# Seven products for the last pair of batches, and the layers of the pair before it moved behind attention

## The chip, the cores and the metric

The kernel runs on one core of a Trainium2 chip. Its engines work side by side, each through its own queue in order: TensorE (PE in the profile, with its weight loads as PEld), VectorE (DVE), ScalarE (ACT), GpSimd (POOL) and SyncE (SP), which only issues transfers. GpSimd issues the indirect transfers (gathers and scatters by a list of row numbers). Engines wait for each other by semaphores. The metric is the device time of one execution in microseconds; the kernel before takes 687.97 us (median of 3 runs, 686.82 to 688.27).

## The reference, cut to what matters

Attention comes first, with the queries averaged in pairs, for 8 batches of 8 heads, 1152 keys, and heads of 64:

```
q_pool = q.reshape(B, H, S // 2, 2, D).mean(axis=3)          # 576 queries
attn   = softmax(q_pool @ k^T / sqrt(D))                     # 576 x 1152
x      = (attn @ v), heads side by side                      # (8, 576, 512)
```

Then each batch sends its 128 best rows through two layers, and the other rows are passed on as they are:

```
scores = einsum('bsd,d->bs', x, w_gate)
for b in range(B):
    top_idx = argpartition(-scores[b], 128)[:128]
    h  = maximum(x[b, top_idx] @ w1, 0)                      # 128 x 1024
    ye = h @ w2                                              # 128 x 512
    out[b, top_idx] += sigmoid(scores[b, top_idx])[:, None] * ye
```

So a batch's layers need its chosen rows, the choice needs the scores of all its 576 rows, and the scores need all of its attention. All arithmetic is in float32; the profile shows each float32 matmul as two instructions.

## The kernel before, in words

**Attention.** The work goes through 32 pairs of heads (`pairs`, batch by batch, four pairs each), each in two halves of 288 queries. The loop in `run` counts 64 halves with `h`. For a half, TensorE does 72 matmuls for the scores (line L869), from which ScalarE makes exponentials into a tile `p` (L876), and one half later 72 matmuls of exponentials by values (`weighted`, L887). GpSimd adds the exponentials of two thirds of the keys (L908), VectorE folds both parts to sums (`folded`, L913, twice a half, and L923), and transposes the drained result (`drained`, L966). VectorE also transposes keys and queries of the pair after the next (`prepare_pair`, L770 and L774). `p` has two buffers.

**Routing.** When a batch's last pair has been scored (`scored`), a generator `routed` is put on the list `routing`. Each `yield` ends a piece of it. `units` runs a piece at one of three places in a half ("mid", "sums", "end"), the place being given by the value that the piece before yielded. The pieces in order: the line of scores (L1068), its spreading to all partitions and to columns, comparisons of each row's score with all others (L1152, L1161, L1171 on VectorE, by tile of 128 rows) which give ranks, a transfer of the ranks to memory and back to every partition (`row_rank`, `lines`, L1201 and L1205, 640 KB), the search for the row of each rank (L1236), the gather of the chosen rows from the output (L1263), their transposition (`xeT`), and the layers.

For batches 0 to 6 the line of scores goes by way of memory (`row`, L1094, read back by L1097 to L1099). For batch 6 it is first merged over the partitions by a matmul (L1083). For batch 7 nothing of this goes by memory: VectorE spreads the line over a diagonal (L1113), two matmuls give it to all partitions (L1124, copied by L1133), five small transposes give its columns (`columns`, L679), and after the ranks a product with matmuls (L1213, L1222) gives the row numbers directly. Batch 7's rows are transposed by TensorE (L1308), the other batches' by a transfer to memory and back (`copy`, L1276 and L1292) and VectorE.

**Layers.** Batches 0 and 1, 2 and 3, 4 and 5 go through the layers as pairs (`layers_of_two`). The rows of a pair, and a weight matrix, are each cut into a two by two block of quarters, and `seven_products` makes the product of both from seven products of quarters instead of eight (L1452). For this there are sums of quarters: of the weights (`tw`, made once and kept in memory, with room in the chip for one layer's at a time, `load_sums`, L730) and of the rows (`input_sums` on GpSimd, L1418). ScalarE copies the products out of PSUM (L1460) and VectorE adds them (seven additions, L1465). Batches 6 and 7 (`b >= self.paired`) each go through `layers`: for layer 1, 32 products of 128 by 128 by 128 (L1327, with ReLU L1335), for layer 2, 8 products with 512 columns (L1347), for batch 7 in two parts of 256 columns.

**Output.** Attention's rows are stored by SP (`stored`, L1024, four transfers a pair). The changed rows are scattered over them by GpSimd (`written`, L1394), one scatter a batch, for batch 7 one for each part of 256 columns. All of them write one tensor of the output, of which `written` names the rows from the first to the end of its batch.

**The end, before.** The first layer of batches 4 and 5 is run within attention (at half `h` = 60). Behind attention the order is written out by hand at the end of `run`: `old` is the rest of batch 6's routing and layers, `older` the second layer of batches 4 and 5, and `new` batch 7's routing and layers; `pieces(unit, n)` runs n pieces. `normalized` merges the last pair's sum by a matmul (L989), and `counted` and `outside` count the softmax sums that are out of bounds, on which a branch to another version of the kernel depends (not taken here).

```
        pieces(new, 1)
        pieces(old, 1)
        for half in (halves[-3], halves[-1]):
            self.divided(half["pair"])
            self.stored(half["pair"])
        pieces(older, 2)
        pieces(new, 1)
```

In this way TensorE has the second layer of 4 and 5, then the layers of 6, to do while batch 7 is routed by the other engines.

Of the kernel before, what the change touches and what calls it, by code (L numbers as in the profile page):

```python
# [13 lines left out]
G = 3  # L14
# [520 lines left out]
class _Plain:  # L535
# [10 lines left out]
    def __init__(self, ctx, tc, q, k, v, moe_w_gate, moe_w1, moe_w2, capacity, out):  # L546
# [48 lines left out]
        self.paired = self.B - 2 - self.B % 2  # L595
        self.tw = self.const.tile([P, 4, self.ND // 2 * self.F // 2], F32, name="tw")
        self.tw_kept = {}
# [70 lines left out]
    def line_of_scores(self):  # L668

        line = self.ffn.tile([P, self.NT * P], F32, name="sc_row", bufs=1)  # L670
        self.nc.gpsimd.memset(line[0:1, self.Sp :], 0.0)
        return line

    def columns(self, to, line):

        nc = self.nc
        ps = self.banks()[:, 0, 0 : self.NT]
        for t in range(self.NT):
            nc.tensor.transpose(  # L679
                ps[:, t : t + 1], line[0:1, t * P : (t + 1) * P], self.ident[0:1, 0:1]  # L680
            )
        nc.scalar.copy(to[:, :], ps)

# [50 lines left out]

    def load_pair(self, b, hp):

        nc = self.nc
        kb = self.load.tile([P, self.KB, BLK], F32, name="kb")
        qb = self.load.tile([P, self.QB, 2, BLK], F32, name="qb", bufs=1)
# [318 lines left out]
    def routed(self, b, part):  # L1058
# [13 lines left out]
        if b < self.B - 1:  # L1072

            yield mid
            if b < self.B - 2:
                groups = self.side_by_side(line)
                yield True
                total = self.added(groups)
            else:
                yield True  # L1080
                total = self.small.tile([BLK, self.QB], F32, name="total", bufs=3)
                ps = self.banks()[:, 0, 0 : self.QB]
                nc.tensor.matmul(  # L1083
                    ps,
                    lhsT=self.merge.rearrange("p g j -> p (g j)"),
                    rhs=line[:, :],
                    start=True,
                    stop=True,
                )
                nc.scalar.copy(total[:, :], ps[0:BLK, :])  # L1090
            sc_row = ffn.tile([P, NT * P], F32, name="sc_row", bufs=1)
            row = self.dram.tile([Sp], F32, name="row")
            nc.gpsimd.memset(sc[:, NF:], 0.0)
            nc.sync.dma_start(row.rearrange("(i n) -> i n", i=BLK), total[:, :])  # L1094

            def reads():
                nc.sync.dma_start(sc_row[:, 0:Sp], _rows_of(row[:], P))  # L1097
                nc.sync.dma_start(sc[:, 0:NF], row[0 : NF * P].rearrange("(t p) -> p t", p=P))
                nc.sync.dma_start(  # L1099
                    sc[0 : self.TAIL, NF:], row[NF * P :].rearrange("(t p) -> p t", p=self.TAIL)  # L1100
                )

            if b < self.B - 2:
                self.behind_keys.append(reads)
            else:
                reads()
            yield True
            if b < self.B - 2:
                yield True
        else:  # L1110

            diag = ffn.tile([P, self.QB, BLK], F32, name="lines", bufs=1)
            nc.vector.tensor_tensor(  # L1113
                out=diag[:, :, :],
                in0=line[:, :].unsqueeze(2).broadcast_to([P, self.QB, BLK]),
                in1=self.same[:, :].unsqueeze(1).broadcast_to([P, self.QB, BLK]),
                op=ALU.mult,
            )
            yield True
            sc_row = self.line_of_scores()  # L1120

            halves = [self.banks()[:, 0, 0 : self.HALF] for _ in range(2)]
            for s, ps in enumerate(halves):
# [343 lines left out]
    def layers_of_two(self, tokens):  # L1467
# [12 lines left out]
        for _ in self.input_sums(a, s):  # L1480
            pass
# [279 lines left out]
```

## Time and profile before

| what | value |
|---|---|
| median of 3 runs | 687.97 us (686.82 to 688.27) |
| profiled execution, its own time | 687.04 us |
| its span | 685.3 us |
| TensorE busy | 676.5 us (99%) |
| VectorE busy | 564.9 us (82%) |
| GpSimd busy | 516.9 us (75%) |
| ScalarE busy | 458.5 us (67%) |
| transfers | 101.21 MB, mean 148 GB/s |
| share of the chain that ended last: TensorE | 90% |
| granted TensorE clock | 0.997 |

Busy shares are averages over the span. The chain of work that ended last is followed back from the last instruction, at each step to what released it or to the instruction before it on its engine. In the timeline a row gives start, duration, engine, line, operation, what it writes and reads, its shape, how many instructions are merged in it, and in square brackets how long the engine stood idle before it and what released it. TensorE's rows are pipelined and their ends are modelled. Times are in microseconds from the start of the span.

### The profile page before, as it was taken

The numbers are of one execution on the slowest core, as the hardware profiler recorded it, in microseconds if no ns is written. First come the engines' busy times: TensorE is split into PE (matmuls) and PEld (weight loads), VectorE is DVE, ScalarE is ACT, GpSimd is POOL, SyncE is SP. The second block draws the span as 40 slices with busy tenths as digits, with TensorE's granted clock in tenths as the row PEclk, the third lists the DMA queues.
The fourth block names the chain that finished last, engine by engine and source line by source line (L and its number), as shares of the span: only waits on it lengthen the run. The fifth ranks groups of instructions, "written<-read, shape, count | busy, mean of one in ns | idle before, by whom it ended". The sixth has DMA issues, their size and how long they took to land.

```text
span 685.3 us, 23541 instructions
## 1 busy us (share of the span) xinstructions
PE 676.5 (99%) x9972; PEld 450.9 (66%) x9972; DVE 564.9 (82%) x842; ACT 458.5 (67%) x998; POOL 516.9 (75%) x503
## 2 busy tenths in 40 slices
PE   8999999999999999999999999999999999999996
PEld 6666666666666568676666657767657665866875
DVE  3878998999999986787699996696879999688830
ACT  5677777777877783848787776583877777576220
POOL 4788888879887883857998788393999889559241
PEclk9999999999999999999999999999999999999998
DMA  8889889849986886744989687572788959344311
GB/s 157 163 179 195 217 185 195 161 91 192 206 179 108 174 156 105 193 88 85 226 192 160 139 165 158 114 175 51 166 197 185 162 123 194 71 116 119 81 47 36
DMA packets 395570, 101.21 MB, mean 148 GB/s; under 512 B 375744, under 2 KB 379712, under 8 KB 394176
## 3 DMA queue, kind: packets, MB, share of 16 engines
q1 hardware_dynamic: 393920, 95.13, 67.0%
q0 software_dynamic: 1296, 4.20, 1.9%
q8 instruction: 80, 1.31, 0.8%
q10 hardware_dynamic: 240, 0.30, 0.2%
q14 instruction: 34, 0.28, 0.1%
HBM read 81.97 MB, written 17.62 MB: 145 GB/s over the span
## 4 chain that ended last, share of the span: by engine, by line
PE 90%; POOL 4%; issue 2%; DMA 2%; DVE 1%; ACT 1%; ACTq 0%; POOLq 0%; DVEq 0%
PE ps L869 39%; PE ps L887 38%; PE ps L1452 11%; POOL acc L908 2%; PE ps L1327 1%; DMA out_dram<-xe,index 1%; POOL xe L1512 1%; DMA p<-in_q_dram 1%; POOL out_dram L1394 1%; POOL qp L767 0%; DMA out_dram<-lines,index_part 0%; POOL prod L976 0%; ACT p L876 0%; DVE kT L770 0%; POOL x L1013 0%
## 5 line engine op out<-in xcount | busy, mean ns | idle before, releaser
L876 ACT ACTIVATE p<-ps 128x576 f32<-128x576 f32 x576 | 321.0, 696 | 4.3 <-PE ps L869 4.0
L908 POOL TENSOR_TENSOR acc<-p 128x576 f32<-128x576 f32 x192 | 275.9, 1464 | 27.9 <-ACT p L876 27.6
L869 PE MATMUL ps<-qT,kT 64*64 64x288 f32 x4608 | 292.9, 403 | 1.6 <-DVE qT L774 0.9
L887 PE MATMUL ps<-p,v_sb 64*64 64x288 f32 x4608 | 291.4, 403 | 0.0
L869 PEld LDWEIGHTS ps<-qT,kT 64*64 64x64 f32 x4608 | 174.6, 133 | 107.4 <-ACT p L876 17.6
L887 PEld LDWEIGHTS ps<-p,v_sb 64*64 64x64 f32 x4608 | 174.1, 133 | 105.4 <-ACT p L876 14.0
L913 DVE TRANSPOSE_TENSOR_REDUCE fold<-p 128x54 f32<-128x1728 f32 x64 | 126.0, 1969 | 27.4 <-ACT p L876 26.8
L913 DVE TRANSPOSE_TENSOR_REDUCE fold<-acc 128x54 f32<-128x1728 f32 x64 | 124.5, 1946 | 21.1 <-POOL acc L908 20.8
L895 ACT COPY two<-ps 128x576 f32<-128x576 f32 x64 | 40.8, 637 | 135.1 <-PE ps L887 118.9
L897 POOL TENSOR_TENSOR av<-two 128x288 f32<-128x288 f32 x64 | 51.2, 800 | 81.4 <-ACT two L895 79.9
L770 DVE STREAM_TRANSPOSE kT<-kb 128x1152 f32<-128x1152 f32 x31 | 73.3, 2364 | 0.0
L976 POOL TENSOR_TENSOR prod<-avb,w_gate 128x288 f32<-128x288 f32 x64 | 51.2, 800 | 0.2
L767 POOL TENSOR_TENSOR qp<-qb 128x576 f32<-128x576 f32 x31 | 43.7, 1409 | 4.7 <-DMA qb<-in_q_dram 4.7
L966 DVE STREAM_TRANSPOSE avb<-av 128x288 f32<-128x288 f32 x64 | 28.6, 447 | 20.0 <-POOL av L897 20.0
L953 ACT ACTIVATE sums<-total,tiny 32x18 f32<-32x18 f32 x124 | 38.2, 308 | 3.0 <-DVE total L944 1.1
L1013 POOL TENSOR_TENSOR x<-avb,rec 128x576 f32<-128x576 f32 x30 | 34.7, 1157 | 0.0
L1171 DVE SCALAR_TENSOR_TENSOR pick<-sc_row,gate_sc,before 128x128 f32<-128x128 f32 (+1 forms) x40 | 32.8, 821 | 1.4
L938 ACT COPY groups<-sum 32x36 f32<-32x36 f32 x124 | 27.2, 219 | 1.5
L1035 DVE TENSOR_REDUCE red<-prod 128x9 f32<-128x288 f32 x64 | 27.7, 434 | 0.1
L1460 ACT COPY s<-ps 128x256 f32<-128x256 f32 (+1 forms) x27 | 11.4, 446 | 20.9 <-PE ps L1452 20.9
L923 DVE TENSOR_REDUCE sum<-fold 128x18 f32<-128x108 f32 x64 | 21.9, 342 | 2.2
L1460 ACT COPY hT<-ps 128x512 f32<-128x512 f32 (+1 forms) x15 | 7.9, 544 | 23.2 <-PE ps L1452 21.3
(136 smaller groups left out, 496.0 us busy)
## 6 DMA issues: line engine op xcount, KB each, us to landing
kb<-in_k_dram SPq DMA_DIRECT2D x124, 144.0 KB
qb<-in_q_dram SPq DMA_DIRECT2D x124, 144.0 KB
v_sb<-in_v_dram SPq DMA_DIRECT2D x31, 576.0 KB
tw<-tw SPq DMA_DIRECT2D x10, 1024.0 KB
out_dram<-x SPq DMA_DIRECT2D x128, 72.0 KB
lines<-row_rank SPq DMA_DIRECT2D x7, 640.0 KB
w<-in_moe_w_dram SPq DMA_DIRECT2D x8, 512.0 KB
tw<-tw SPq DMA_DIRECT2D x8, 512.0 KB
```

Source lines behind the costliest of these rows:

```text
L767: nc.gpsimd.tensor_tensor(out=qp[:, :, :], in0=pair["q"][:, :, 0, :], in1=pair["q"][:, :, 1, :], op=ALU.add)
L770: nc.vector.transpose(kT.rearrange("p (c i g) -> p c g i", c=self.NC, i=BLK), pair["k"].rearrange("p (g c) d -> p c g d", c=self.NC),)
L869: nc.tensor.matmul(sc[keys, j, 0:n], lhsT=pair["kT"][rows, c * P + keys.start : c * P + keys.stop], rhs=pair["qT"][rows, qs], start=True, ...
L876: nc.scalar.activation(p[:, c // G, c % G, :, :], sc[:, :, 0:n], AF.Exp, scale=self.scale)
L887: nc.tensor.matmul(av[j * self.D : (j + 1) * self.D, e, 0:n], lhsT=half["pair"]["v"][keys, j, c, :], rhs=half["p"][keys, c // G, c % G, j, :],
L895: nc.scalar.copy(two[:, :, :], av[:, :, 0:n])
L897: nc.gpsimd.tensor_tensor(out=half["av"][:, :], in0=two[:, 0, :], in1=two[:, 1, :], op=ALU.add)
L908: nc.gpsimd.tensor_tensor(out=acc[:, u, :], in0=units[:, 0, u, :], in1=units[:, 1, u, :], op=ALU.add)
L913: nc.vector.tensor_reduce(fold[:, a, :], of.rearrange("p u (m d) -> p (u m) d", d=BLK), AX.X, ALU.add, apply_transpose=True,)
L953: self.nc.scalar.activation(tot[rows, :], pair["total"][:, j * self.QB : (j + 1) * self.QB], AF.Identity, bias=self.tiny[0:BLK, 0:1],)
L976: self.nc.gpsimd.tensor_tensor(out=pair["prod"][:, ns, :], in0=pair["avb"][:, ns, :], in1=self.w_gate[:, hp : hp + 1, :].broadcast_to([P, ...
L1452: nc.tensor.matmul(args[0], lhsT=args[1], rhs=args[2], start=k == 0, stop=k == n - 1)
```

## The change

Four parts, all around the end of attention:

- `layers_of_two` stops for batches 4 and 5 after the sums of the input (`self.left`); both their layers are run behind attention. The marks "hidden", `waiting` and `place` that had put layer 1 inside and layer 2 outside are gone.
- Batches 6 and 7 no longer go through `layers` but, as a pair, through `first_layer` and `second_layer`, in seven products each. Here the order of the seven is another than in `seven_products`: those that need no sums first, and VectorE adds products straight from PSUM. For layer 2, `load_last_sums` loads the kept sums of the weights in four transfers of 512 KB into tiles of keys and queries during the last two pairs, so that the sums of layer 1 can stay in `tw` for both pairs.
- Batch 7's line of scores is spread by four ScalarE copies and one reduction and goes by way of `row` in memory, as the earlier batches' does; the diagonal and `columns` are gone. Batch 6's line is made by the same copies instead of the matmul. Batch 7's two small gate operations go from GpSimd to VectorE.
- The end is a function of its own, `ending`, with a new order: attention's last half, layer 1 of 4 and 5 between the pieces of batch 7's routing, the four sums of its layer 2 on GpSimd, layer 2 with the rest of the routing, then layer 1 and layer 2 of 6 and 7 with their sums on VectorE. The scatters come in the order 4, 5, first half of 6's columns, all of 7, second half of 6's columns.

The diff, cut to its core:

```diff
-            if b < self.B - 2:
-                groups = self.side_by_side(line)
-                yield True
-                total = self.added(groups)
-            else:
-                yield True
...
+        groups = self.side_by_side(line)
+        if b < self.B - 1:
             yield True
+        total = self.added(groups)
+        sc_row = ffn.tile([P, NT * P], F32, name="sc_row", bufs=1)
+        row = self.dram.tile([Sp], F32, name="row")
+        nc.gpsimd.memset(sc[:, NF:], 0.0)
+        nc.sync.dma_start(row.rearrange("(i n) -> i n", i=BLK), total[:, :])
...
-            self.columns(sc, sc_row)
...
+        small = nc.vector if b == self.B - 1 else nc.gpsimd
...
             if b >= self.paired:
-                yield mid
-                yield from self.layers(token)
+                self.last_tokens.append(token)
...
+        if tokens[1]["b"] + 1 == self.paired:
+            self.left = tokens, a, s
+            return
         yield "mid"
...
+    def load_last_sums(self):
...
+        for room in rooms:
+            to = (self.row(room) if len(room.shape) > 2 else room)[:, 0:n]
+            self.nc.sync.dma_start(to, self.tw_kept[2][:, len(self.last_sums), :])
...
+    def first_layer(self, a, s, c, m):
...
+        copy(u, product(a11, b11))
+        hidden(c11, u, product(a12, b21))
+        copy(w, product(s1, t1))
+        self.add(u, u, product(s2, t2))
+        self.add(w, w, u)
+        ps = product(s3, t3)
+        hidden(c22, w, ps)
+        self.add(u, u, ps)
+        hidden(c12, w, product(s4, b22))
+        hidden(c21, u, product(a22, t4))
...
+    def second_layer(self, a, s):
...
+        for of, by in ((a11, b11), (a12, b21), (a22, t4), (s1, t1), (s2, t2), (s3, t3), (s4, b22)):
+            yield self.product(2, of, by, self.banks()[:, 0, :])
...
+    def ending(self, halves, old):
...
+        self.gated(halves[-3])
+        pieces(old, 1)
+        self.weighted(halves[-1])
+        self.drained(halves[-1])
+        self.multiplied(halves[-2])
+        self.multiplied(halves[-1])
+        self.scored(halves[-3])
+        self.gated(halves[-2])
+        pieces(layer, 1)
+        self.normalized(last)
+        self.gated(halves[-1])
+        self.scored(halves[-1])
+        _, new, _ = self.routing.pop()
+        pieces(old, 1)
+        pieces(new, 1)
+        pieces(layer, 2)
+        for of in (halves[-3]["pair"], last):
+            self.divided(of)
+            self.stored(of)
+        pieces(layer, 3)
+        pieces(new, 1)
+        pieces(layer)
+        room = self.ffn.tile([P, 4, 512], F32, name="s", bufs=1).rearrange("p a n -> p (a n)")
+        s = self.four_sums(nc.gpsimd, c, room)
...
+        layer = self.second_layer(c, s)
+        for to in at[0:2]:
+            copy(to, next(layer))
+        pieces(new, 2)
+        for to in at[2:5]:
+            copy(to, next(layer))
+        pieces(new, 1)
+        pieces(old)
+        for to in at[5:7]:
+            copy(to, next(layer))
+        low = self.counted()
...
+        pieces(layer, 1)
+        pieces(new)
+        self.four_sums(nc.vector, a, room)
...
+        ps = next(layer)
+        add(v, v, ps)
+        add(u, u, ps)
+        scaled(to[3], v, seven, to[3])
+        add(y, y, u)
+        scaled(to[2], y, seven, to[2])
+        self.written(seven, seven["index"])
+        scaled(to[1], next(layer), six, z)
+        self.written(six, index[1], 1, 2)
```

## The prediction

> **What bounds the kernel now.** I read the page's busy shares first (busy us, share of the span, instructions), then the chain of work that ended last (start, us, what), then the timelines around the places that the diff touches.
>
> ```profile
> PE 676.5 (99%) x9972; PEld 450.9 (66%) x9972; DVE 564.9 (82%) x842; ACT 458.5 (67%) x998; POOL 516.9 (75%) x503
> ```
>
> The chain where the diff takes work out:
>
> ```profile
> 582.44 0.33 PE ps L1083 x2
> 582.77 4.53 PE ps L869 x72
> 587.29 12.70 PE ps L1452 x112
> ...
> 626.52 8.73 PE ps L887 x144
> 635.25 1.93 PE ps L1452 x8
> ```
>
> TensorE has work all the time, and the chain follows it almost to the end. 12.70 us of the first layer of batches 4 and 5 (L1452, 112 matmuls, seven products of 1.81) stand inside attention; the last weighted sum ends at 635.25. From there TensorE runs without a gap to 679.58. The granted clock is 1.00 up to 665, so matmul rows can be carried over.
>
> The edges of the last stage, and the queue that ends the kernel, from the timeline:
>
> ```profile
> 635.52 0.34 DVE L923 TENSOR_REDUCE sum<-fold 128x18 f32<-128x108 f32 x1
> 637.01 0.31 PE L989 MATMUL ps<-sum,merge 128*128 128x36 f32 x2
> ...
> 660.68 1.03 POOL L1394 DMA_INDIRECT out_dram<-xe,index  x1 [0.28 <-POOL xe L1512]
> 664.27 1.00 POOL L1394 DMA_INDIRECT out_dram<-xe,index  x1 [1.12 <-DMA out_dram<-xe,index]
> 676.99 0.98 POOL L1394 DMA_INDIRECT out_dram<-lines,index_part  x1 [8.07 <-DVE index_part L1381]
> 680.38 0.97 POOL L1394 DMA_INDIRECT out_dram<-lines,index_part  x1 [2.42 <-DVE lines L1356]
> ```
>
> Two things to see. VectorE finishes the sum of the last half only 0.6 us after attention ends on TensorE. And a scatter to the output is not started before the one ahead of it has landed: the second line of L1394 waits for a DMA, and the chain shows the landing 2.79 us after the first one's start and 0.80 more until the next starts.
>
> The last row that carries a step is a comparison (L1171) on VectorE, beside POOL's sums and without them:
>
> ```profile
> 607.71 1.43 DVE L1171 SCALAR_TENSOR_TENSOR pick<-sc_row,gate_sc,before 128x128 f32<-128x128 f32 x1
> 610.17 0.39 DVE L1171 SCALAR_TENSOR_TENSOR pick<-sc_row,gate_sc,before 128x128 f32<-128x128 f32 x1
> 617.84 1.51 DVE L1171 SCALAR_TENSOR_TENSOR pick<-sc_row,gate_sc,before 128x128 f32<-128x128 f32 x1
> ```
>
> **1. TensorE's own work.** Before, the moved and removed parts take 12.70 (layer 1 of 4 and 5) + 0.33 (merge of batch 6's line, L1083) + 44.33 (635.25 to 679.58) = 57.36 us. After: two pairs, each with 12.70 for layer 1 and 12.57 for layer 2 (the chain's four L1452 pieces after 635.25: 1.93 + 3.53 + 1.73 + 5.38), 50.54; merge 0.14 (L989), choice of rows 1.15 (L1222), transposes 0.63 (L1308), count 0.19 (L1541): 52.65. Gone are the plain layers (7.3 and 7.1 per batch by L1327 and L1347) and batch 7's line on TensorE (L1124 1.03, L679 0.40). TensorE gains 4.7 us. Attention then ends at 635.25 - 13.03 = 622.2, and without any wait TensorE would end at 674.9.
>
> **2. The cover that goes.** Those 12.70 us were time in which VectorE caught up: idle 3.07 and 1.39 us before its two folds at 588.59 and 591.96, 1.48 at 595.78, 1.67 at 606.20. Its queue from the first fold's partner (ends 593.94, bound by POOL as before) to the sum of the last half, in start-to-start times of the trace, without the seven additions L1465 (0.69 each): sum, totals, two transposes, the drained half 3.9, ranks of batch 6 5.3: 603.2. Next half 8.9, of which 1.16 was one comparison beside POOL, which now is done by then: 611.0. Next half's folds and drain 5.2: 616.2. Then it needs the 640 KB of batch 6's ranks: the write went out at 620.94 and the search that needs them began at 627.96, 7.0 later; so 618.0. Two searches: 3.3 as seen, 1.85 by their shortest rows; 2.6 taken, 620.6. Last half 4.55: 625.2. TensorE has its merge (L989) in line behind one product, at 622.2 + 1.8 = 624.1. Everything behind the merge waits with it: **1.2 us**. Ends: 623.3 (shortest searches and a transfer sooner by 1.2), no wait; 627 (another tie comparison beside POOL), 3.
>
> **3. Batch 7's line by way of memory.** I count from the sum of the last half, S. Drain, gate reductions and part take 3.6 (635.86 to 639.74 now); four ScalarE copies 0.92 and one reduction: S+4.9. The row's write to its first read: 1.42 by the row at 620.94 and its follower at 622.36, quiet queues; 3.97 (585.31 to 589.28) under full DMA load. The load is light by then, so 1.42. Three reads are issued over 0.9, and the last lands 3.0 after its issue (one such read held POOL's gate once, 362.12 to 365.4): S+10.3. Ahead of them on SP are batch 6's copy and its reading (637.83 and 640.14 now), done some 3 us before. Behind them are eight stores, 6.1 us of issue, landed by S+17, and the gather that needs them comes at S+23: free. The four loads of layer 2's sums (2 MB, as before) go out during the last two pairs and are not needed for 20 us; if late, the first product with a sum is S+16.5.
> VectorE's own queue fills the same time: two divisions 1.42, six additions of 0.69 up to the sixth product, S+10.4. So the detour costs nothing here; without that cover it would cost the difference to the matmul way (639.74 to 644.36, 4.6): about 2. PSUM as an addition's source I bound by 0.69 and 0.8 (L1356, 0.48 for 256).
>
> **4. Choice of rows of batch 7.** Ranks of tiles 0 and 1 take 2.65 and the gate 0.25: S+13.3; one addition 0.69; tiles 2 to 4, rank and choice 5.6 (647.03 to 652.56 now): S+19.7 alone. But POOL does the four sums of layer 2 (1.28 each) from S+14.9 to S+20, beside three comparisons and the choice. One or two of three are stretched by about 1.1 in the trace: 0 to 3.4, taken 1.6, so S+21.3 and 0.15 to TensorE. TensorE arrives at S + 0.3 + 6 x 1.81 + 5 x 1.80 = S+20.2. Wait: **1.25 us** (0 to 3). The sums themselves are ready 0.3 ahead of their products.
> The Trainium skill, SBUF — State Buffer, section "SBUF: two separate sides", says that a VectorE operation with two SBUF inputs and a GpSimd operation lock each other out for a whole instruction; L1171 at 607.71 agrees (1.43) and at 610.17 doesn't (0.39, with POOL busy). By the rule each of the four operations would wait half of a POOL sum, 4 x 0.64 = 2.6 instead of 1.6, and the result would be 1 us later.
> The gather then has 3.6 + 1.8 of products to land in; 654.11 to about 658.1 now, 4.0. Free; a landing of 5.5 instead of 3.5 would cost 0.6.
>
> **5. The pair 6 and 7.** Layer 1 takes additions of 0.69 on VectorE, about 9 us in 11 us of products; layer 2 starts with three products that need no sum, 5.4 us, and the first sum is ready 2.1 us after layer 1. No wait. Edits at nothing: batch 6's line by four ScalarE copies of 0.22 instead of a matmul, ScalarE being 67% busy and the line not needed for 12 us; the gate's two small operations on VectorE (0.1 each, in step 4); the count of odd sums (1.6 on VectorE after the choice, with 5 us until the transposes). TensorE's end: 625.2 + 50.9 + 1.25 = 677.4.
>
> **6. The end.** Now: the last scatter starts 0.80 after TensorE's end and the span ends 4.92 later. After: batch 7's whole rows are scattered after the sixth product, behind five VectorE operations of 0.41 to 0.48 (2.3) and 0.28 of start: 2.57 after that product. Batch 6's second half is scattered next, and its start needs that landing: 2.79 or 3.09 (rows of 660.68 and 667.93) and 0.80. That is 2.57 + 2.95 + 0.80 - 1.80 = 4.5 after TensorE's end, instead of 0.8: **3.7 us lost**. The scatters of 4, 5 and the first half of 6 stand in the same queue, each held by the one ahead, and are done 3 us before.
>
> **Sum.** 677.4 + 4.5 + 4.92 = 686.8 against 685.3: -4.7 + 1.2 + 1.25 + 3.7 = +1.5. The profiled execution took 687.04, 0.9 below the median of 687.97; on the median 689.5. A measurement of this kernel tells about 0.2% (1.4 us) from no change, so the sum lies on that edge.
>
> **The rivals.**
> *The last scatter is not held* (faster). If batch 7's scatter and batch 6's last do not wait for each other, only POOL's 1.0 of issue stands between them: start 1.87 after TensorE's end, 2.6 us less, so -1.2, and -3.6 with no wait in steps 2 and 4. It decides from a hold of 2.2 us: below that, instead of 3.75, the kernel is no slower than before. For it: row 680.38 names VectorE. Against: 664.27 names the DMA, and the chain has the landing at 679.49 ahead of 680.38. 15%, two thirds of it faster by over 0.2%.
> *VectorE is in time* (no change). Searches without POOL and ranks earlier: S by 624.1, and comparisons unstretched. Both waits go: -0.9. For it: POOL has less to do in those halves, its four sums of layer 2 (5.1 us) being gone. Against: before 574, where no layers stood between, VectorE was busy 42.77 of 44 us. 20%, a quarter of it faster.
> *VectorE's backlog is larger* (slower). Two more stretched comparisons and ranks that land late give 3 for the merge and 3 for the choice, +5. If exponentials wait for the folds as well, more; there the margin is 2 us (folds done 607.4, exponentials from 609.4). 25%.
> The sum's own case has 40%, with a range of its own from -0.5 to +3.
>
> **How the numbers follow.** Faster by over 0.2%: 10 of the first rival, 5 of the second, 5 of the sum's case, mis-sized by 3: 20. Within: 5, 15 and 15: 35. Slower: 20 of the sum's case and 25 of the third rival: 45. The range goes from -3.6 (nothing waits) to +5: 684.4 to 693.
>
> **What would show it.** TensorE: no L1452 matmuls in the halves before the end, attention done by 622; a gap before the merge named for VectorE's sum, about 1 us; one before the choice of rows, with comparisons of 1.4 us under POOL's sums; end near 677. POOL: the last scatter 3.5 us or more behind the one ahead. I am wrong if the last scatter follows within 2 us, if the merge never waits, or if attention itself slows.

## The result, and the profile after

The changed kernel takes 691.38 us (median of six, 689.88 to 692.67) against 687.45 of the kernel before (six, 686.41 to 688.37): a ratio of 1.0054, 95% interval 1.0037 to 1.0071, so some 3.7 us slower. The profiled execution has a span of 689.6 us (685.3 before) and took 691.44. The forecast was 689.5, a loss of 1.5: right in sign, but less than half of the loss in size, and it is the size that taught most.

The busy shares of the changed kernel, as on the page shown of before:

```profile
PE 673.4 (98%) x9953; PEld 455.7 (66%) x9953; DVE 575.0 (83%) x868; ACT 458.9 (67%) x1004; POOL 516.7 (75%) x500
```

TensorE is busy 3.1 us less, in a span 4.3 longer: about 7 us more stand around it. Its timeline from the end of attention to the transposes (start, us, line, matmuls; in brackets the idle time ahead and who ended it):

```profile
624.86 2.05 PE L1442 MATMUL ps<-xeT,w 128*128 128x128 f32 x16
627.24 0.38 PE L991 MATMUL ps<-sum,merge 128*128 128x36 f32 x2 [0.32 <-DVE sum L925]
...
645.16 1.89 PE L1452 MATMUL ps<-qb,s 128*128 128x256 f32 x8
648.54 1.33 PE L1186 MATMUL ps<-meta,pick 128*128 128x2 f32 x10 [1.49 <-DVE pick L1177]
649.81 3.06 PE L1452 MATMUL ps<-kb,s 128*128 128x256 f32 x8
652.66 2.56 PE L1452 MATMUL ps<-w,s 128*128 128x256 f32 x8
655.05 1.95 PE L1442 MATMUL ps<-p,w 128*128 128x128 f32 x16
```

Three things. Attention ends at 624.86 (635.25 before, 622.2 forecast). The merge waits 0.32, the choice of rows 1.49: both waits of the forecast are there, the first much smaller. And the two products behind the choice take 5.24 from start to start (649.81 to 655.05), where a product at full clock needs 1.73. No wait is shown there; they are simply slow. The granted clock in four stretches of 1 us says why (a row gives the stretch, its length, TensorE's busy time and instructions, the granted clock, and the transfers):

```profile
650.00:651.00 1.00, 1.00 (x5) 0.79 0.00 0
651.00:652.00 1.00, 1.00 (x4) 0.50 0.09 16
652.00:653.00 1.00, 1.00 (x4) 0.50 0.79 217
653.00:654.00 1.00, 1.00 (x4) 0.50 0.12 45
```

The clock is at a half from about 650.6 to 654.0, 3.4 us, which costs 1.7. In the kernel before it is at 1.00 up to the end of TensorE's work.

A second loss stands in attention, where batch 6's line is added up by four ScalarE copies (one line of ScalarE's timeline, then one of TensorE's):

```profile
576.91 0.85 ACT L940 COPY groups<-line 32x18 f32<-32x18 f32 x4 [0.98 <-DVE line L1070]
...
578.36 2.84 PE L871 MATMUL ps<-qT,kT 64*64 64x288 f32 x40 [1.26 <-ACT p L878]
```

The copies wait for VectorE's line, the exponentials of the next half stand behind them in ScalarE's queue, and TensorE waits 1.26 for PSUM to come free.

The end, from TensorE's and POOL's timelines, and the same place in the chain of work that ended last:

```profile
678.83 1.89 PE L1452 MATMUL ps<-w,p 128*128 128x256 f32 x8
```

```profile
681.31 0.98 POOL L1303 DMA_INDIRECT out_dram<-lines,index  x1 [6.53 <-DVE lines L1624]
684.83 0.98 POOL L1303 DMA_INDIRECT out_dram<-xe,index_part  x1 [2.53 <-DMA out_dram<-lines,index]
```

```profile
681.31 2.74 DMA out_dram<-lines,index
...
684.83 0.98 POOL out_dram L1303
```

TensorE's last product ends at 680.7 (678.83 + 1.89). The last scatter starts 4.1 us later, held by the landing of the one ahead of it; before it started 0.80 after TensorE's end. So the span's 4.3 are 1.1 of TensorE's end (679.58 to 680.7), 3.3 of this hold, and 0.15 less behind it (4.77 instead of 4.92).

### The profile page after: what moved, and what is told of

The parts are those of the page before. It is cut to its first block, busy times and chain, and to the rows that moved or that the text cites. A ratio compares the mean times of both kernels' runs of the same rounds, so it can differ in the third digit from the quotient of the medians.

```text
span 689.6 us, 23548 instructions
## 1 busy us (share of the span) xinstructions
PE 673.4 (98%) x9953; PEld 455.7 (66%) x9953; DVE 575.0 (83%) x868; ACT 458.9 (67%) x1004; POOL 516.7 (75%) x500
## 3 DMA queue, kind: packets, MB, share of 16 engines
q8 instruction: 79, 1.29, 0.8%
## 4 chain that ended last, share of the span: by engine, by line
PE 76%; DVE 7%; DMA 6%; POOL 5%; issue 3%; ACT 2%; SPq 1%; ACTq 0%; POOLq 0%; DVEq 0%
PE ps L871 33%; PE ps L889 32%; PE ps L1361 7%; PE ps L1442 3%; POOL acc L910 3%; DVE fold L915 2%; ACT p L878 1%; DMA xe<-out_dram,index 1%; DVE kT L772 1%; DMA kb<-in_k_dram 1%; PE ps L1452 1%; POOL out_dram L1303 1%; DMA lines<-row_rank 1%; DVE pick L1125 1%; DVE pick L1135 1%
## 5 line engine op out<-in xcount | busy, mean ns | idle before, releaser
L871 PEld LDWEIGHTS ps<-qT,kT 64*64 64x64 f32 x4608 | 177.1, 132 | 108.3 <-ACT p L878 20.5
L889 PEld LDWEIGHTS ps<-p,v_sb 64*64 64x64 f32 x4608 | 176.9, 133 | 102.9 <-ACT p L878 14.3
L776 DVE STREAM_TRANSPOSE qT<-qp 128x576 f32<-128x576 f32 x31 | 23.0, 741 | 0.0
L1125 DVE TENSOR_SCALAR_CACHE_REDUCE pick<-sc_row,gate_sc 128x576 f32<-128x576 f32 (+4 forms) x40 | 21.6, 539 | 0.3
```

Source lines behind the costliest of these rows:

```text
L871: nc.tensor.matmul(sc[keys, j, 0:n], lhsT=pair["kT"][rows, c * P + keys.start : c * P + keys.stop], rhs=pair["qT"][rows, qs], start=True, ...
L889: nc.tensor.matmul(av[j * self.D : (j + 1) * self.D, e, 0:n], lhsT=half["pair"]["v"][keys, j, c, :], rhs=half["p"][keys, c // G, c % G, j, :],
```

## The experiments

A ratio is always to the kernel before, on the same chip and beside it. c0_after, e1, e2 and e3 ran in one job; b0, e5, e6 and e7 in another; e4 and e8 in a third; e9 and c1 in a fourth.

**The changed kernel again (c0_after)**, no edit.

> The changed kernel once more, beside its variants. In its first profile TensorE was already 1.5 us late at 346.8 us, before any instruction that the change touches, behind a gather that landed late (POOL's scatter waited 1.2 us for it). If that is chance, this profile has no such gap or has it elsewhere, and the median stays between 690.0 and 692.5 (3 to 5 us above the kernel before). If it belongs to the change, the gap is there again at the same place.

Measured: 691.45 us, 1.0054 (1.0036 to 1.0071). The loss stands. But its profiled execution has a span of 688.1, and there TensorE's timeline behind the very same wait reads:

```profile
648.73 1.33 PE L1186 MATMUL ps<-meta,pick 128*128 128x2 f32 x10 [1.50 <-DVE pick L1177]
649.99 1.99 PE L1452 MATMUL ps<-kb,s 128*128 128x256 f32 x8
651.82 1.89 PE L1452 MATMUL ps<-w,s 128*128 128x256 f32 x8
653.55 1.95 PE L1442 MATMUL ps<-p,w 128*128 128x128 f32 x16
```

The two products take 3.56 from start to start, 1.68 less than in the first profile, and the span is 1.5 shorter. The same wait costs clock in one execution and none in the other. I come back to that with e8 and e9.

**The kernel before again (b0_before)**, no edit.

> The kernel before once more. Five profiles of the changed kernel and its variants all show TensorE waiting 0.4 to 1.6 us at 346 us for a transposition (L776), behind a gather that took 5.0 to 5.6 us to land; the one profile of before shows 4.5 and no wait there. The instructions up to there are the same on every queue. If chance, this profile has the wait at 346 too, and its TensorE ends within 0.5 us of the one that is known or later. If it belongs to the change (other addresses of buffers or code), there is no wait at 346 again.

Measured: 687.14 us, 1.0000 (0.9991 to 1.0010), span 685.3. TensorE waits 0.81 at 346 us, where the first profile had no wait, and not at 512, where that one had 0.95. The sum of the waits at these two places is 0.8 to 1.0 in the two profiles of the kernel before and 0.9 to 2.1 in the three of the changed one (2.08, 0.99 and 0.9). All of this lies ahead of the change, with the same instructions on every queue. Over all twelve profiles of the changed kernel and its variants the sum is 0.9 to 2.6, in ten of them above 1.0; that the changed kernel leans to the longer waits is likely from this, but with two profiles of the kernel before it isn't shown.

**The order at the end (e1_order).** In layer 2 of the last pair the seventh product is taken fifth and the sixth product last, so that batch 6's half is scattered ahead of batch 7's rows.

```diff
-        for of, by in ((a11, b11), (a12, b21), (a22, t4), (s1, t1), (s2, t2), (s3, t3), (s4, b22)):
+        steps = ((a11, b11), (a12, b21), (a22, t4), (s1, t1), (s2, t2), (s3, t3), (s4, b22))
+        if last:
+            steps = [steps[i] for i in (0, 1, 3, 4, 6, 2, 5)]
+        for of, by in steps:
```

> The last pair's second layer in another order: the product that ends batch 6's second half (s4 b22) stands fifth instead of seventh, and the one that batch 7's rows wait for (s3 t3) last; batch 6's last scatter goes out two products before the end. Theory (the last scatter is held by batch 7's until that has landed): the last scatter then starts about 2.2 us after TensorE's end instead of 4.25, and lands 0.3 later for its 512 columns: 1.7 us faster than the changed kernel. Rival (scatters hold nobody, the end is bound by TensorE and VectorE's additions): no more than 0.5 us either way, since the products and nearly all the additions are the same.

Measured: 689.59 us, 1.0021 (1.0003 to 1.0040), so 0.33% below the changed kernel of the same job (2.3 us by the ratios, 1.9 by the medians). The last product on TensorE, and the last two scatters on POOL:

```profile
678.79 1.89 PE L1452 MATMUL ps<-kb,p 128*128 128x256 f32 x8
```

```profile
678.03 0.98 POOL L1303 DMA_INDIRECT out_dram<-xe,index_part  x1 [3.28 <-DVE xe L1627]
682.79 0.98 POOL L1303 DMA_INDIRECT out_dram<-lines,index  x1 [3.78 <-DVEq L1806]
```

The last scatter now waits for VectorE and not for a landing; it starts 2.1 after TensorE's end instead of 4.1. The order of the products decides whether the hold is paid.

**The scatter of batch 7 left out (e4_no_seven).**

```diff
-        self.written(seven, seven["index"])
```

> The scatter of batch 7's whole rows is left out, so the update of batch 7 is missing from the output; everything else is done. Theory (the last scatter of batch 6 is held until the one ahead of it has landed): with the one ahead gone, the last scatter starts about 1.1 us after TensorE's last product (two operations on VectorE and POOL's start) instead of 4.25, at 681.7 where the changed kernel has 684.83, and the time is 3.1 us below the changed kernel's, about 688.3 on its 691.4. Rival (no hold, the scatter of batch 7 only takes POOL's 1.0 of issue ahead of it): at most 0.7 us below the changed kernel.

Measured: 688.01 us, 1.0017 (1.0003 to 1.0030). There was no changed kernel in that job; against its 1.0054, and against the 1.0036 that it had in another job (c1 below), this is 1.3 to 2.5 us less. TensorE's last product and the last two scatters:

```profile
679.48 1.89 PE L1452 MATMUL ps<-w,p 128*128 128x256 f32 x8
```

```profile
674.42 0.98 POOL L1303 DMA_INDIRECT out_dram<-xe,index_part  x1 [4.97 <-DVE xe L1624]
682.36 0.98 POOL L1303 DMA_INDIRECT out_dram<-xe,index_part  x1 [6.95 <-DVEq L1802]
```

With nothing ahead of it the last scatter starts 1.0 after TensorE's end: the hold is worth 3.1 in the trace, as expected, and more than the 0.7 that POOL's issue could explain. In this execution the clock was at a half for 6.8 us behind the choice of rows, not for 3.4, and TensorE ended 0.65 later than in the changed kernel's first profile, so that its span is only 2.2 shorter. Why the medians show less than 3.1 can't be told without a changed kernel in the job.

**Batch 6's line by the merge matmul again (e2_six_matmul).**

```diff
-        groups = self.side_by_side(line)
...
+        if b == self.B - 2:
...
+            nc.tensor.matmul(
+                ps,
+                lhsT=self.merge.rearrange("p g j -> p (g j)"),
+                rhs=line[:, :],
+                start=True,
+                stop=True,
+            )
+            nc.scalar.copy(total[:, :], ps[0:BLK, :])
```

> Batch 6's line is merged by a matmul again, as in the kernel before; all else as changed. Theory (the four ScalarE copies wait for VectorE's line ahead of the next half's exponentials and hold them, and through them TensorE, by 1.26 us at 578): that gap goes and 0.33 us of matmul comes back: 0.9 us faster than the changed kernel. Rival (ScalarE has room, and the gap in the profile is the same chance as that at 346): within 0.3 us of the changed kernel, and a gap of ScalarE's before the scores of that half stays.

Measured: 689.88 us, 1.0030 (1.0015 to 1.0045): some 1.6 below the changed kernel of the job, with intervals that overlap. On TensorE's timeline the 72 matmuls of that half run through, with no wait in them:

```profile
575.33 4.54 PE L871 MATMUL ps<-qT,kT 64*64 64x288 f32 x72
```

The wait of 1.26 was that of the copies. (The same wait is 1.30 in both repeats of the changed kernel and 2.0 in two other runs.)

**The gate's last steps early (e3_gate).** The exponential and the addition of one, for batch 7, are moved from behind the last rank to its first tiles.

```diff
+            if b == self.B - 1 and t == 0:
+                nc.scalar.activation(gate[:, :], gate[:, :], AF.Exp, scale=-1.0)
```

> Batch 7's exponential of the gate and the addition after it stand among the first comparisons, before POOL's four sums, instead of behind the last comparison. Theory (that small addition took 1.22 instead of 0.1 us since it stood behind one of POOL's sums, and TensorE waited 1.5 us for the choice of rows behind it): the choice is ready 1.1 us sooner, TensorE waits 0.4: 1.1 us faster than the changed kernel. Rival (another of VectorE's two-input operations takes its place behind POOL's sum, the choice itself above all): within 0.3 us, and the wait of 1.5 stays.

Measured: 690.52 us, 1.0034 (1.0019 to 1.0048), which overlaps with the changed kernel's 1.0054. The span is 689.7 (689.6), and TensorE waits 1.41 for the choice (1.49). VectorE's timeline has the reason:

```profile
640.47 0.17 DVE L1149 TENSOR_SCALAR gate<-gate 128x5 f32<-128x5 f32 x1
...
646.31 1.96 DVE L1185 TENSOR_TENSOR pick<-token_line,rank 128x640 f32<-128x640 f32 x1
```

The small operation now takes 0.17 instead of 1.22, but the comparison behind it takes 1.96 instead of 1.29: it ran into the POOL sum that the small one had sat out. Taking one operation out from under a POOL operation handed the wait to the next. So the trace has it as the rival said. The times don't decide: by the medians the kernel is 0.9 below the changed one of the job, nearer to the theory's 1.1 than to the rival's 0.3, with intervals that overlap.

**Batch 7's line over TensorE again (e5_columns).** The row is spread by a diagonal, two halves of matmuls and five transposes, as before the change; the path over memory is left out for batch 7.

```diff
+            diag = ffn.tile([P, self.QB, BLK], F32, name="lines", bufs=1)
...
+                nc.tensor.matmul(
+                    ps,
+                    lhsT=self.ones[:, :],
...
+                nc.tensor.transpose(
+                    ps[:, t : t + 1], sc_row[0:1, t * P : (t + 1) * P], self.ident[0:1, 0:1]
+                )
```

> Batch 7's line of scores goes over TensorE again (diagonal, two matmuls, five transposes, placed between the products of layer 1 of 4 and 5), not by way of memory; all else as changed. Theory (the detour by memory lies beside VectorE's additions and costs nothing): TensorE gets 1.4 us more and waits some 0.5 for the diagonal, the wait for the choice of rows shrinks from 1.5 to 0.4: 1.2 us slower than the changed kernel (0 to 2). Rival (the routing of batch 7 is late by its transfers): the choice comes 2 us or more earlier and the kernel is faster.

Measured: 689.6 us, 1.0034 (1.0023 to 1.0046). It is not slower than the changed kernel: a miss. On TensorE's timeline:

```profile
630.06 1.21 PE L1113 MATMUL ps<-lines,ones 128*128 128x288 f32 x4 [0.31 <-DVE lines L1102]
...
648.19 1.33 PE L1217 MATMUL ps<-meta,pick 128*128 128x2 f32 x10 [0.46 <-ACT acc L1606]
649.46 1.99 PE L1483 MATMUL ps<-kb,s 128*128 128x256 f32 x8
```

TensorE has some 1.4 us of matmuls more and 0.31 of waiting, and gets 1.03 back at the choice, where it waits 0.46 instead of 1.49: 0.7 lost, not 1.2. And the clock stays whole in this profile, which against the changed kernel's first one is worth 1.7 and turns the sign. The path over memory relieves TensorE of work at a place where it then stands and waits for VectorE; whether it gains anything, times of different jobs (1.0034 here, 1.0036 and 1.0054 for the changed kernel) don't tell.

**Layer 1 of batches 4 and 5 within attention again (e6_early).**

```diff
-            self.left = tokens, a, s
+            yield "mid"
+            hidden = [ffn.tile([P, self.NFC, P], F32, name="hT") for _ in tokens]
...
+            yield from self.seven_products(1, a, s, c, rest, lines)
```

> Layer 1 of batches 4 and 5 stands within attention again, as in the kernel before; the pair 6 and 7 and all else as changed. Theory (what covers batch 7's routing is the layers of 4 and 5, and a pair can't start until batch 7's rows are there): five products of layer 2 end 9.3 us after the last half's sum, the choice of rows comes 18.9 after it; TensorE waits 9.5 us there instead of 1.5, VectorE is in time for the merge: 7.5 us slower than the changed kernel. Rival (TensorE has the same 52.7 us to do whatever the order, and the place of layer 1 doesn't matter): within 1 us.

Measured: 702.73 us, 1.0223 (1.0208 to 1.0238): 1.7% or some 12 us over the changed kernel's 1.0054 (of another job), where 7.5 were expected. TensorE around the choice of rows:

```profile
644.19 1.89 PE L1460 MATMUL ps<-qb,s 128*128 128x256 f32 x8
657.17 2.35 PE L1186 MATMUL ps<-meta,pick 128*128 128x2 f32 x10 [11.09 <-DVE pick L1177]
659.45 3.78 PE L1460 MATMUL ps<-kb,s 128*128 128x256 f32 x8
```

Without the seven products of layer 1 behind attention there is nothing to do while batch 7's ranks are made: the wait grows from 1.49 to 11.09, 9.6 of the span's 10.0. So the move of layer 1 behind attention is what makes the rest of the change bearable at all. The clock falls to a half 3.9 us into that wait and stays there until 663.7: the ten tiny matmuls take 2.35 instead of 1.33, the next product 3.78 instead of 1.99.

**The choice of rows one product later (e8_late).**

```diff
-        for to in at[2:5]:
+        for to in at[2:6]:
             copy(to, next(layer))
         pieces(new, 1)
         pieces(old)
-        for to in at[5:7]:
+        for to in at[6:7]:
```

> The choice of batch 7's rows stands one product of layer 1 later on TensorE (behind the sixth instead of the fifth product after the ranks of batch 7 begin); nothing else is changed. Theory (TensorE waits 1.5 us for the choice because VectorE and POOL are late, and one product of 1.8 covers that): the wait of 1.49 before the choice goes, the gather starts about 0.3 us later and the transposes wait about 0.3 for it, so about 1.2 us below the changed kernel, 690.2 on its 691.4. Rival (the choice is late by whatever stands ahead of it, and the wait only moves to the transposes behind the gather): the transposes wait 1.2 or more and the time is within 0.3 us of the changed kernel's.

Measured: 687.53 us, 1.0007 (0.9995 to 1.0020), level with the kernel before: 2.0 to 3.2 us less than the changed kernel (1.0036 and 1.0054), where the wait alone would be 1.2. On TensorE's timeline:

```profile
646.15 1.89 PE L1452 MATMUL ps<-kb,s 128*128 128x256 f32 x8
648.29 1.33 PE L1186 MATMUL ps<-meta,pick 128*128 128x2 f32 x10 [0.25 <-DVE pick L1177]
649.55 1.99 PE L1452 MATMUL ps<-w,s 128*128 128x256 f32 x8
...
653.59 0.72 PE L1275 MATMUL ps<-ident,lines 128*128 128x128 f32 x4 [0.27 <-DMA lines<-out_dram,index]
```

The wait is 0.25, the gather is waited for 0.27, as expected, and the product behind takes 1.99: in this profile the clock doesn't fall. 1.24 - 0.27 + 1.7 = 2.7 lies within the 2.0 to 3.2 measured. How much is gained hangs on the changed kernel's clock: from the start of the merge to TensorE's end e8's profile takes 51.13 us, the changed kernel's 53.48 with the fall (the first one) and 51.81 and 52.34 without it (c0 and c1).

**The wait filled with useless matmuls (e9_filled), and the changed kernel beside it (c1_after).** Nothing is moved; ahead of the choice TensorE multiplies weights that nobody asked for.

```diff
+                for k in range(6):
+                    nc.tensor.matmul(
+                        fill, lhsT=by[:, k % 2, 0:P], rhs=by[:, k % 2, :], start=(k == 0), stop=(k == 5)
+                    )
```

> Ahead of the choice of batch 7's rows TensorE gets six matmuls of 128x256 whose result nobody reads (0.216 each by the rows of 8 in 1.73, so 1.30 in all), and they end 0.2 before the choice can begin. Nothing the kernel needs is done sooner. Theory (the wait of 1.5 and the 1.3 of two-column matmuls behind it let the granted clock fall to a half, and the two products behind them then take 5.2 from start to start instead of 3.55, as in the changed kernel's profile and not in the repeat's): the granted clock stays at 1.00 from 645 to 660 and the two products take 3.55, so the time is about 1.7 us below the changed kernel's in this job wherever that one's clock falls. Rival (the clock doesn't hang on this gap, or what it costs is hidden behind something later): the time is the changed kernel's within 0.5.

> The changed kernel once more, on the chip and in the job of the filled one, so that the two stand side by side: 1.0054 of the kernel before. By the theory of the clock its granted clock is below 1.00 in the 10 us behind the choice of rows in some executions and not in others, the first being some 1.5 us longer; by the rival the clock says nothing of the time.

Measured: filled 689.98 us, 1.0036 (1.0020 to 1.0051); changed 689.93, 1.0036 (1.0013 to 1.0058). The time is the same, so by the time alone the rival has it. TensorE's timeline of the filled kernel says what happened:

```profile
647.16 2.75 PE L1187 MATMUL ps<-w 128*128 128x256 f32 x12
649.75 1.26 PE L1192 MATMUL ps<-meta,pick 128*128 128x2 f32 x10
650.94 1.99 PE L1458 MATMUL ps<-kb,s 128*128 128x256 f32 x8
652.77 1.89 PE L1458 MATMUL ps<-w,s 128*128 128x256 f32 x8
654.50 1.95 PE L1448 MATMUL ps<-p,w 128*128 128x128 f32 x16
```

The clock stayed whole and the two products take 3.56. That alone confirms nothing, since it stayed whole in the changed kernel's profile beside it (c1) too, behind a wait of 1.95. And I had misread the size: the 8 of a product are four matmuls in two parts, so six are 12 lines and 2.6 us, not 1.3, and they delay the choice by about 0.9 (VectorE was done with it at 648.70). From the start of the merge to TensorE's end the filled kernel takes 52.75: 0.7 less than the changed kernel's profile with the fall, 0.4 and 0.9 more than the two without. So this run neither confirms the theory nor refutes it; the filler was too long.

The changed kernel's executions differ among themselves. Each has a mean granted clock and a span. Over the 27 of three jobs (the first result, c0 and c1):

```
mean granted clock   executions   span, mean (lowest to highest)
0.996                    10       687.4 (685.9 to 688.7)
0.993 and 0.994           9       689.0 (688.1 to 689.9)
0.992 and below           8       691.1 (689.6 to 694.3)
```

Executions with a lower mean are longer, by 1.6 and by 3.7 us, as the theory has it; 3.4 us at a half clock lower the mean by 0.0025, and the profile with the fall has 0.994, the two without it 0.996. The filled kernel has 0.995 or more in 11 of its 12 executions, the changed one in 10 of 27. But the mean is no sure sign of the fall, because it takes in the tail behind TensorE's last product as well. The two profiles of the kernel before, without a fall ahead of that, have 0.997 and 0.999 at the same span of 685.3: the clock falls 2.2 us behind the last product in one and 4.8 in the other. e4's profile, with 6.8 us at a half, has 0.994 too. And the eleven executions of the kernel before at 0.995 and 0.996, beside c0, c1 and e8, are 1.6 to 2.3 longer than the others of their job. So the table goes with the theory and doesn't show it; in how many of the 27 executions the clock fell behind the choice is not known.

**All that pays, together (e7_all).** e1's order (with the two halves of batch 7 made ready ahead of the last product, two operations behind it instead of four), e2's matmul, e8's later choice. The end of it, where it differs from e1:

```diff
+        scaled(to[3], v, seven, to[3])
+        scaled(to[2], y, seven, to[2])
         ps = next(layer)
-        add(v, v, ps)
-        scaled(to[3], v, seven, to[3])
-        add(y, y, ps)
-        scaled(to[2], y, seven, to[2])
+        scaled(to[3], ps, seven, to[3])
+        scaled(to[2], ps, seven, to[2])
```

> Three edits together: batch 6's last scatter two products earlier, with the additions for batch 7's last rows made ahead of the last product (two operations behind it instead of five); batch 6's line merged by a matmul again; and the choice of rows one product later, so that TensorE has a product to do in the 1.5 us in which it waited. Theory: 2.6 + 0.9 + 0.6 (between 0.2 and 1.1, since the gather then starts 0.3 later and may be waited for) = 4.1 us faster than the changed kernel, so level with the kernel before (-1 to +1). Rival (the waits only move on): no faster than the best of the single edits, 1.5 us slower than before.

Measured: 683.27 us, 0.9935 (0.9921 to 0.9949): 4.5 us faster than the kernel before and some 7 to 8 faster than the changed one, which ran in other jobs (1.0036 and 1.0054). TensorE's timeline, then POOL's last scatters:

```profile
624.73 0.38 PE L991 MATMUL ps<-sum,merge 128*128 128x36 f32 x2
...
646.11 1.29 PE L1199 MATMUL ps<-meta,pick 128*128 128x2 f32 x10
...
651.39 0.72 PE L1288 MATMUL ps<-ident,lines 128*128 128x128 f32 x4 [0.29 <-DMA lines<-out_dram,index]
...
673.64 1.89 PE L1465 MATMUL ps<-kb,p 128*128 128x256 f32 x8
```

```profile
672.87 0.98 POOL L1316 DMA_INDIRECT out_dram<-xe,index_part  x1 [3.29 <-DVE xe L1640]
676.72 0.98 POOL L1316 DMA_INDIRECT out_dram<-lines,index  x1 [2.86 <-DVEq L1819]
```

TensorE ends 5.2 sooner than in the changed kernel (675.5 against 680.7). 2.0 of that are there at the end of attention: 1.26 of the copies, less 0.33 for the matmul that comes back, 0.5 less of the waits at 346 and 512 us, 0.4 of a wait in the first 10 us, and 0.2 left over. Then come 0.32 of the merge, 1.49 of the choice and 1.68 of the clock, less 0.29 for the gather. The last scatter starts 1.2 after TensorE's end instead of 4.1. That is nearly twice the gain that I expected (4.1); 1.7 of the difference, against the first profile, are the clock behind the wait, which I hadn't counted.

## Why the prediction was right, and where it was off

The sum's own case came true in sign and in its two largest terms, the 4.7 of work saved and the hold at the end (3.7 forecast, 3.3 found). Its total did not: it was 2.8 short in the profile (686.8 forecast, 689.6 found), because TensorE ended at 680.7 instead of 677.4. The loss of 4.3 lies outside the sum's own range, which ended at 3; the whole range, up to 5, holds it only because it was drawn out for the rival of the larger backlog, which didn't happen. That is luck. So is that one of the signs of being wrong, "if attention itself slows", appeared and did no harm to the forecast: the slowing made the kernel slower still.

**TensorE's own work (step 1).** Right: from the end of attention it has 52.4 us of work in the changed kernel (55.9 to its end, less 0.32, 1.49 and 1.68); forecast 52.65. The end of attention was forecast at 622.2 and came at 624.86. Of the 2.7, 1.26 are the exponentials behind the copies, 1.1 the longer waits at 346 and 512 us, which belong to no part of the change that I can name, and 0.3 are left over.

**The edit costed at nothing (step 5).** This failed: "batch 6's line by four ScalarE copies of 0.22 instead of a matmul, ScalarE being 67% busy and the line not needed for 12 us". Who needs the line was the wrong question. What counts is who stands behind the copies in ScalarE's queue while they wait for their own input, and those were exponentials that free PSUM for TensorE. It cost 1.26, and e2 took it away (for 0.33 of matmul that comes back).

**The cover that goes (step 2).** The wait for the merge was mis-sized: 1.2 forecast, 0.32 found. The sum of the last half was ready 2.2 after attention's end, not 3.0: attention ended 2.7 later than forecast, the sum only 1.9 later. VectorE's part of it stands in its timeline:

```profile
619.79 1.47 DVE L1200 SCALAR_TENSOR_TENSOR pick<-lines,token,token_line 128x640 f32<-128x640 f32 x1 [1.45 <-DMA lines<-row_rank]
```

It stood idle for the ranks of batch 6, which landed at 619.8 and not at 618.0. That is nearly all of the 1.9; the searches and the last half took what was forecast, within 0.2. So it was the ranks, and not VectorE's own work, that set the sum's time, and the forecast 1.2 came down to 0.32 through delays elsewhere.

**By way of memory (step 3).** The steps are as told: the first read goes out 1.37 after the row's write (1.42 forecast). That it costs nothing held, as far as e5 can tell: 1.0034 without the path, 1.0036 and 1.0054 with it.

**The choice (step 4).** The wait was 1.49 for 1.25; VectorE was done 21.3 us after the sum of the last half, as forecast. On VectorE's timeline two operations are stretched:

```profile
641.71 1.26 DVE L1135 SCALAR_TENSOR_TENSOR pick<-sc_row,gate_sc,before 128x128 f32<-128x128 f32 x1
...
643.99 0.35 DVE L1135 SCALAR_TENSOR_TENSOR pick<-sc_row,gate_sc,before 128x128 f32<-128x128 f32 x1
...
645.58 1.22 DVE L1152 TENSOR_SCALAR gate<-gate 128x5 f32<-128x5 f32 x1
647.11 1.29 DVE L1177 TENSOR_TENSOR pick<-token_line,rank 128x640 f32<-128x640 f32 x1
```

One comparison of five and the gate's addition, some 2.0 in all, for 1.6 forecast. Each of the two began 0.14 to 0.16 into one of POOL's sums (641.55 to 642.82 and 645.44 to 646.78) and ended 0.02 to 0.15 after it; the comparison at 643.99 began 0.17 before the end of a sum and took 0.35. So what an operation pays is what is left of the sum that it starts under. This also sets right how the forecast read the row at 610.17 in the kernel before, as one without a sum and then as one that speaks against the lock of the page that it cites: POOL's sum there ended at 610.42, 0.25 after the comparison began, and the comparison ended 0.14 after it, as the stretched one at 607.71 did (0.15). The row agrees with the lock.

What failed in this step is the sentence on which all rows were carried over, "The granted clock is 1.00 up to 665": it is so in the kernel before, where TensorE doesn't stop, and the change makes it stop. The wait's price was 1.5 and, in the first profile, 1.7 more behind it; of the seven profiles of the changed kernel and its variants with a wait of 1.41 to 1.95 there, five have such a fall and two have none.

**The end (step 6).** Right: the last scatter starts 4.1 after TensorE's end (4.5 forecast, 0.8 before), held by the landing ahead. The rival without a hold fell with the trace, e1 and e4; so did the larger backlog of VectorE, whose merge would have waited 3, and VectorE in time, since the choice does wait.

The span by terms: 1.1 for TensorE's end (-4.7 of work, 1.26 copies, 0.32 merge, 1.49 choice, 1.68 clock, 1.1 longer waits at 346 and 512 us), 3.3 for the hold, -0.15 behind it.

## What to carry to other kernels

A wait on a TensorE that was never idle can cost twice: the wait itself, and what the clock does behind it, here where the first work after it was a handful of tiny matmuls. A full product of the kernel's own work put there (e8) took most of the wait away, and no fall was seen behind it; useless matmuls that lasted longer than the wait (e9) brought nothing that the times show. An operation on an engine that isn't the bound is free only if nothing urgent stands behind it in that engine's queue while it waits for its own input. Where scatters to one output hold each other, order the work so that the last product feeds the last scatter and the one ahead has long landed.

## What the runs showed of the hardware that I had not expected

The granted clock fell to 0.50 behind 1.49 us of idleness and 1.33 us of two-column matmuls, for 3.4 us, in the first profile of the changed kernel; behind 1.95, 1.90 and 1.41 us of idleness, for 3.4 us each, in e1's, e2's and e3's; and behind 1.94, for 6.8, in e4's. It stayed at 1.00 behind 1.50 in c0's and 1.95 in c1's, with the same matmuls after it; and it stayed at 1.00 behind idle times of 1.26 to 2.03 in attention, where full matmuls follow at once. Where the wait at this place was under 0.5 (e5, e7, e8, e9), it didn't fall. So it isn't the length of the gap alone: among these profiles it falls in some and not in others, and only where little is multiplied after the gap. In e6, with 11.09 us of idleness, the clock was at a half for 13.6 us. The three lengths, 3.4, 6.8 and 13.6, are one, two and four times the same step.

The Trainium skill, TensorE: Matmul & The Clock Gate, Part 1 on the HAM clock gate, says that the clock follows TensorE's activity in windows of about 3.4 us which run freely, and drops to a half after an idle one. The step of 3.4 us here, and a fall that comes and goes at the same place, agree with it. But in the changed kernel's first profile no window was idle throughout, as the gap with its tiny matmuls was 2.8 us long; and behind the last product of the kernel before the clock fell after 2.2 us of idleness in one profile and 4.8 in the other. In e6's wait, where it fell after 3.9, a whole window was idle.

A VectorE addition on 128x5 numbers took 1.22 us when it began 0.14 us into a POOL sum of 1.34, against 0.17 and 0.16 away from one (e3, e6). When it was moved, the comparison that took its place was stretched by 0.67 instead (e3).
